# RWKV-7 recurrence with a SoLU block on one core: key scaling on VectorE, and a written order for the first half of the program

## The chip, the core and the metric

The kernel runs on one core of a Trainium2 chip. The core has five engines, each with its own in-order queue: TensorE (PE; its weight loads are shown as PEld), VectorE (DVE), ScalarE (ACT), GpSimd (POOL) and SyncE (SP), which here only issues DMA transfers. An instruction that waits for a semaphore holds everything behind it on its own engine and nothing on the others. The metric is the device time of one execution in microseconds, and its median over the runs shown.

## The reference

Two blocks follow each other. The first is a recurrence over 768 time steps for 4 batches and 8 heads with head size 40; the second is a feed-forward block with a SoLU activation, a layer norm and a second product, over the 3072 tokens that come out of the first.

```python
for t in range(S):                                   # S = 768, state is D x D, D = 40
    y[:, :, t] = einsum('bhd,bhde->bhe', rt, state)
    Sa = einsum('bhde,bhe->bhd', state, at)
    state_decay = state * wt[:, :, None, :] - einsum('bhd,bhe->bhde', Sa, bt)
    state = state_decay + einsum('bhd,bhe->bhde', vt, kt)
x = y.transpose(0, 2, 1, 3).reshape(B * S, H * D)    # (3072, 320)
h = x @ w_in                                         # (3072, 1024)
e = exp(h - max(h)); sm = e / (sum(e) + 1e-9)
solu = h * sm
ln = (solu - mean(solu)) / sqrt(var(solu) + 1e-6) * g_ln
out = ln @ w_out                                     # (3072, 320)
```

The weights `w_in`, `w_out` and `g_ln` come as 64-bit floats and the rest as 32-bit.

## The kernel before

**Chunks.** Time is cut into chunks of 64 steps. A work item i is one chunk of two batches, so that 128 partitions hold 2 x 64 steps; there are N = 24 items, and items i and i + 2 belong to the same two batches, whose state passes from one to the next. Inside an item the recurrence is a triangular system, solved by an explicit inverse of blocks of 32.

**What one item goes through**, with the line of the function in the code:

- its keys and values are loaded (`load_keys` L318 for w, b, a, k; `load_values` L328; `load_r` L335);
- the logarithm of the decays is summed along time on TensorE and exponentiated on ScalarE, once as `ei` and once inverted as `inv` (`logged` L349, `decay` L353);
- `scaled` (L386) multiplies the keys b and k by `inv` into the tile `kb`, with one GpSimd instruction for each of the two (L393);
- the a keys and the scaled b keys are transposed on TensorE (`front` L421, `front_b` L429), and `norm` (L465) multiplies them; its result `nt` is stored to DRAM;
- the results of two items together are read back as `blk` (`spread` L488) and inverted on VectorE (`invert` L495), in 30 steps that a schedule strews between other work. The first step is L502 to L508, and a late step is two products (L516) and two additions (L519). The inverse goes to DRAM (`uu_dram`, L525), and comes back for each item (`bring` L529) as `tu` and `uh`; `flip` (L542) transposes `tu` in 32 x 32 blocks on VectorE;
- `attend_kv`, `attend_r`, `scores`, `couple`, `close`, `carried`, `driven`, `solved`, `read` and `summed` (L574 to L711) make the item's output and its new state. `scores` has two maskings on VectorE (L444, `psi` and `lv`), `couple` multiplies by the flipped `tu`, `solved` has one masking (`lu`), `read` accumulates in two halves, `summed` and `leave` (L714) write the new state and store the output x through DRAM;
- `left` (L732) reads x back transposed, `hidden` (L740) multiplies it with `w_in` in five parts into the PSUM tile `h`, `highest` (L756) takes its maximum, `exped` (L763) the exponential on ScalarE, `weighed` (L771) the product with h on VectorE, `spreadof` (L780) the square on ScalarE and the power on GpSimd (L792), `folded` (L794) transposes the result on TensorE (`plnT`), and `output` (L845) multiplies it with `w2` (`po`) and stores it.

**The weights** are narrowed from 64 to 32 bits on the chip in 13 parts (5 of `w_in`, 8 of `w2`). A part is loaded by `land` (L161) and narrowed by `split` (L188) in three stages: the beginning on VectorE (L196, L197), the scaling on ScalarE (L199 to L206) and the end on VectorE (L208 to L210). When all are there, `centred` (L262) takes the mean out of `w2`.

**What sets the order.** The order of instructions on each engine is the order in which the Python code emits them. Four items are prepared first; then a loop runs over slots i = -1 to 26. In slot i the front of item i + 5 is made, item i + 1 is scored, item i is solved and read, and the feed-forward block works on item c = i - 2. From slot 5 on the slots have their steady form. The table `plans` (L896) says, slot by slot, where steps of inverses and stages of narrowing are strewn on VectorE; a number stands for so many steps, b, s and f for the three stages.

**Queues.** Most loads are issued from SyncE. GpSimd issues the loads of r, the stores of x and of most `nt`, the reads of most blocks, and a few of the early loads of b, a and k, all in one queue with its scalings. ScalarE issues the constants, the first b keys and the rows of g.

The scaling before is one line:

```python
for n in names:
    j = H * (n == "b")
    nc.gpsimd.tensor_tensor(out=kb[:, j:j + H, 0:D], in0=d["raw_" + n], in1=heads(d["inv"]), op=ALU.mult)
```

Of the kernel before, what the change touches and what calls it, by code (L numbers as in the profile page):

```python
# [17 lines left out]
P = 128  # L18
C = 64
# [9 lines left out]


# [23 lines left out]
def kernel(  # L54
# [93 lines left out]
    turn = dict(X="B", Y="C")  # L148

# [62 lines left out]
    begun, scaling, ended = [], [], []  # L212

    def begin_narrow():
        load, part = next(parts)
        assert load < len(lands) + 3 or len(ended) >= len(lands)
        begun.append((load, part, split(*part)))
        next(begun[-1][-1])

    def scale_narrow():  # L220
        scaling.append(begun.pop(0))
        next(scaling[-1][-1])

    def end_narrow():
        load, part, rest = scaling.pop(0)
        for _ in rest:
            pass
        ended.append(load)
        if part is landed[load][-1] and load in LANDS_NEXT:
            land(LANDS_NEXT[load], nc.gpsimd)  # L230

    def vector(plan):

        for word in plan.split():
            if word in "bsf":
                dict(b=begin_narrow, s=scale_narrow, f=end_narrow)[word]()
            else:
                some(int(word.strip("o")), (i + 2) // GRP if "o" in word else N)

    def turn_g(pg):  # L240
        nc.tensor.transpose(out=pg[:, 0:NF], in_=g_rows, identity=ident[0:NF, 0:NF])
        for x, y in zip(g_cols, (0, -20, -36)):
            nc.scalar.mul(out=x, in_=pg[:, 0:NF], mul=2.0 ** y)
# [7 lines left out]
    def mean_more(t, lo, hi, begun=None):  # L251
        if begun is not None:
            nc.tensor.matmul(t[:, 0:DM], lhsT=ident, rhs=begun, start=True, stop=False)
        mean_part(t, lo, hi, begun is None)
        return mean_kept(t)
# [85 lines left out]
    def by_value(i):  # L341
# [3 lines left out]
        for x, y in ((v_t[0][:, :, 0:D], d["lv"][:, :, C:]), (r_t[0][:, :, 0:D], d["raw_r"])):  # L345
# [7 lines left out]
    def decay(i, t=None):  # L353
# [3 lines left out]
        if "lw" not in d:  # L357
            logged(i)
# [3 lines left out]
        def evict():  # L362
            nc.scalar.activation(out=ei_t[0][:, :, 0:D], in_=heads(t), func=AF.Exp)
            inv = d["inv"] = two.tile([P, DM], FP32, tag="inv", name="inv", bufs=4)
            nc.scalar.activation(out=inv, in_=t, func=AF.Exp, scale=-1.0)
        return evict

    def decay_by_halves(i, t):
# [10 lines left out]
        def evict():  # L379
            nc.scalar.activation(out=ei_t[0].rearrange("p (x h) d -> p x h d", x=2)[:, :, :, 0:D],  # L380
                                 in_=t.rearrange("p x (h d) -> p x h d", d=D), func=AF.Exp)
            inv = d["inv"] = two.tile([P, DM], FP32, tag="inv", name="inv", bufs=4)
            nc.scalar.activation(out=inv.rearrange("p (x n) -> p x n", x=2), in_=t, func=AF.Exp, scale=-1.0)
        return evict

    def scaled(i, names="bk"):  # L386
# [4 lines left out]
        for n in names:  # L391
            j = H * (n == "b")
            nc.gpsimd.tensor_tensor(out=kb[:, j:j + H, 0:D], in0=d["raw_" + n], in1=heads(d["inv"]), op=ALU.mult)  # L393
# [65 lines left out]
    def shared_pair(i):  # L459

        if i not in shared:
            shared[i] = pair(turn["Y"], "py")
        return shared[i]

    def norm(i):  # L465
        if not ok(i):
            return
# [6 lines left out]
        nt = d["nt"] = tokens("nt", AHEAD)  # L474
        nc.scalar.mul(out=nt, in_=t[:, :, 4 * Q:4 * Q + 256].rearrange("p b (j c) -> p b j c", j=4), mul=-1.0)  # L475
        n, at = divmod(i, GRP)
        if at == 0:
            blocks[n] = dram.tile([2, 2 * GRP * H, Q, Q], FP32, tag="nt_dram", name="nt_dram")
        for x in range(2):
            for e in range(2):  # L480
                home = C * x + Q * e
                queue = nc.sync if 1 < i < 4 or i == 1 and x else nc.gpsimd
# [5 lines left out]
    def spread(n):  # L488
        nb = two.tile([P, Q, Q], FP32, tag="blk", name="blk")
# [3 lines left out]
        return nb  # L493

    def invert(n):  # L495
        u = two.tile([P, Q // 2, Q], FP32, tag="uu", name="uu")
        flat = u.rearrange("p c t -> p (c t)")
        nc.gpsimd.memset(u[C:P], 0.0)
        nc.gpsimd.memset(flat[C:P, 1::Q + 2], 1.0)
        nb = spread(n)  # L500
        yield
        nc.vector.tensor_tensor(out=u[0:C], in0=nb[0:C, 0::2], in1=above, op=ALU.mult)  # L502
        nc.vector.memset(flat[0:C, 0::Q + 2], 1.0)
        for j in range(1, Q - 1):
# [15 lines left out]
            if j < Q - 2:  # L520
                yield
        inverse[n] = dram.tile([Q, C, Q], FP32, tag="uu_dram", name="uu_dram")
        for y in range(2):
            queue = nc.sync
            queue.dma_start(out=inverse[n][y::2].rearrange("c b t -> b c t"), in_=u[C * y:C * y + C])  # L525
        yield


    def bring(i):  # L529
# [6 lines left out]
        for x in range(2):  # L536
            queue = nc.sync if i or not x else nc.gpsimd
            queue.dma_start(out=d["tu"][C * x:C * x + Q, :, Q:2 * Q], in_=src[0, at, :, x])
        for x in range(2):
# [21 lines left out]
    def close(i):  # L561
        if not ok(i):
            return
# [6 lines left out]
        nc.scalar.copy(out=d["tu"].rearrange("p (h j) c -> p h j c", h=2)[:, :, :, 2 * Q:],  # L570
# [3 lines left out]
    def attend_kv(i, t):  # L574
# [4 lines left out]
        for y, x in enumerate((d["kb"], v_t[0])):  # L579
            turned(t, y, x)  # L580
# [25 lines left out]
    def stated_r(i):  # L606

        if not ok(i) or not where_(i)[1]:
            return
# [6 lines left out]
        for x, part in enumerate((slice(0, HW), slice(HW, C))):  # L616
            nc.scalar.copy(out=state_of(i)[:, x, :, 0:part.stop - part.start].rearrange("p (x q) c -> p q x c", q=2),  # L617
                           in_=by_units(t[:, :, 0:256])[:, :, :, part])

    def scores(i):  # L620
# [3 lines left out]
        t = pair(turn["X"], "ps")  # L624
        for u in in_turn(lambda p, q, g, h: (h, p)):
            p, q, g, h = u
            j = 2 * q + g
            mm(t[half(p), h, j * C:j * C + C], keyed(d["kT"], u), keyed(d["aT"], u))
        for u in in_turn(lambda p, q, g, h: (q, p)):
# [3 lines left out]
        psi = d["psi"] = tokens("psi")  # L633
        masked(psi, by_units(t[:, :, 0:256]))
# [3 lines left out]
    def carried(i):  # L638
# [5 lines left out]
        d["px"] = pair(turn["X"], "px")  # L644
# [21 lines left out]
    def solved(i):  # L666

        if not ok(i):
            return lambda: None
        d = st[i]  # L670
        t = pair(turn["Y"] if i >= LAG else "h", "pu")
# [6 lines left out]
        copy = lambda: nc.scalar.copy(out=o[:, :, :, C:], in_=y[:, :, :, C:])  # L678
        if i < LAG:
            copy()  # L680
# [488 lines left out]
```

## Time and profile before

| | |
|---|---|
| runs, us | 538.32, 538.21, 536.38; median 538.21 |
| span of the profiled execution, us | 536.5 |
| TensorE busy | 480.7 us (90%) |
| VectorE busy | 430.6 us (80%), 1752 instructions |
| ScalarE busy | 314.1 us (59%) |
| GpSimd busy | 227.0 us (42%), 376 instructions |
| mean granted TensorE clock | 0.984 |
| DMA | 63.95 MB, mean 119 GB/s |

The page of a profile gives, for one execution, the busy time of each engine, the same in 40 slices of the span, the chain of work that ended last, followed back from the last instruction, and groups of equal instructions. A row of a group reads: line, engine, operation, output tile <- input tiles, output shape <- input shape and type, count | busy time, mean ns of one | idle time of the engine just before them, and what ended most of it. A row of the timeline reads: start, duration in us, engine, line, operation, tiles, shape, count, and in square brackets the idle time before it and who ended that. SPq and the like are the sequencers that issue DMAs. A duration can overlap the next one's start, so that the time from start to start is a little shorter. A row of the windows reads: stretch, length, and then for PE, PEld, DVE, ACT and POOL the busy time and the number of instructions, the granted clock, the share of the DMA engines, and GB/s. A row of the waits reads: who waited <- for whom: total us, times, longest.

The busy shares are averages over a beginning, in which items are prepared and weights narrowed, a steady part, and an end, so that stages are read apart in what follows.

### The profile page before, as it was taken

Reading aid. Unit: us, or ns where it says so; the run is one execution under the profiler, and the core shown is the slowest. Engines: PE = TensorE matmul, PEld = TensorE weight load, DVE = VectorE, ACT = ScalarE, POOL = GpSimd, SP = SyncE. Lnnn points to the kernel's source line nnn. Section 1 sums busy time; section 2 is a strip of 40 time slices with the busy share of each in tenths; the row PEclk is TensorE's granted clock in tenths of the full one; section 3 lists DMA queues with packets and bytes.
Section 4 is the critical chain, followed back from the end, with each engine's and each line's share of the span. In section 5 each row is a group of like instructions: output and inputs, shape, how many; then the busy total and the mean of one; then the engine's idle time right before and its main releaser. Section 6 shows DMA issues by size and latency. Waiting matters only on the chain.

```text
span 536.5 us, 28053 instructions
## 1 busy us (share of the span) xinstructions
PE 480.7 (90%) x12029; PEld 391.0 (73%) x12029; DVE 430.6 (80%) x1752; ACT 314.1 (59%) x627; POOL 227.0 (42%) x376
## 2 busy tenths in 40 slices
PE   4633775798989999999999999999999999999997
PEld 3522665665878878877887887788778877887766
DVE  4599987999997987997998979979989888544322
ACT  3633466488457566556666665666656555654433
POOL 4577538245253344545445263544445331210300
PEclk9999978799999999999999999999999999999999
DMA  8898889765465566674774776675554551421210
GB/s 149 153 157 160 177 142 206 165 134 124 90 131 120 102 125 138 123 151 96 147 156 104 132 150 121 118 155 109 114 118 102 108 111 43 106 65 29 61 53 24
DMA packets 194475, 63.95 MB, mean 119 GB/s; under 512 B 166840, under 2 KB 186528, under 8 KB 194352
## 3 DMA queue, kind: packets, MB, share of 16 engines
q1 hardware_dynamic: 181232, 41.60, 41.8%
q0 software_dynamic: 10768, 19.95, 15.2%
q8 instruction: 94, 1.54, 1.2%
q10 hardware_dynamic: 2352, 0.62, 0.7%
q14 instruction: 29, 0.24, 0.2%
HBM read 47.96 MB, written 14.16 MB: 116 GB/s over the span
## 4 chain that ended last, share of the span: by engine, by line
PE 73%; DVE 17%; DMA 5%; issue 2%; ACT 2%; SPq 0%; POOL 0%; ACTq 0%; POOLq 0%; DVEq 0%
PE po L285 20%; PE h L285 18%; PE px L285 6%; PE pyo L285 5%; PE py L285 5%; DVE prod L516 4%; PE ps L285 4%; DVE uu L519 3%; PE pu L285 3%; PE plnT L804 2%; PE pb L400 2%; PE pa L400 2%; PE psr L285 2%; PE pkv L400 2%; DMA uu_dram<-uu 1%
## 5 line engine op out<-in xcount | busy, mean ns | idle before, releaser
L285 PE MATMUL h<-w_in,xT 64*64 64x512 f32 (+1 forms) x1064 | 121.7, 551 | 0.7 <-issue 0.7
L285 PE MATMUL po<-w,lnT 128*128 128x160 f32 x768 | 115.2, 304 | 0.0
L516 DVE TENSOR_TENSOR prod<-blk,uu 128x48 f32<-128x48 f32 (+19 forms) x576 | 108.1, 227 | 1.3
L285 PEld LDWEIGHTS po<-w,lnT 128*128 128x128 f32 x768 | 105.5, 190 | 4.7 <-issue 0.8
L519 DVE TENSOR_TENSOR uu<-uu,prod 128x48 f32<-128x48 f32 (+19 forms) x576 | 103.8, 219 | 0.0
L483 POOL DMA_DIRECT2D nt_dram<-nt x86 | 50.8, 597 | 84.5 <-ACT nt L475 76.4
L792 POOL TENSOR_TENSOR rs<-var,mhalf 128x1 f32<-128x1 f32 x24 | 17.6, 734 | 138.2 <-ACT var L791 138.1
L761 DVE TENSOR_REDUCE nmax<-h 128x1 f32<-128x1024 f32 x24 | 29.3, 1219 | 32.9 <-PE h L285 32.9
L285 PEld LDWEIGHTS h<-w_in,xT 64*64 64x64 f32 x1064 | 36.7, 133 | 20.4 <-issue 16.7
L790 ACT ACTIVATE sq<-e,mu 128x1024 f32<-128x1024 f32 x24 | 26.9, 1119 | 24.4 <-DVE e L777 24.4
L444 DVE TENSOR_TENSOR lu<-pu,cst 128x512 f32<-128x512 f32 x24 | 16.5, 686 | 26.6 <-PE pu L285 24.8
L769 ACT ACTIVATE e<-h,nmax 128x1024 f32<-128x1024 f32 x24 | 26.7, 1111 | 17.7 <-DVE nmax L761 17.7
L558 ACT ACTIVATE wy<-py,cst 128x256 f32<-128x256 f32 x24 | 11.4, 474 | 39.2 <-PE py L285 37.1
L311 POOL DMA_DIRECT2D raw_r<-in_r_dram x48 | 33.3, 698 | 0.0
L777 DVE SCALAR_TENSOR_TENSOR e<-h,e 128x1024 f32<-128x1024 f32 x24 | 29.2, 1217 | 4.3 <-ACT e L769 4.1
L508 DVE SCALAR_TENSOR_TENSOR uu<-blk,uu 128x30 f32<-128x30 f32 (+3 forms) x144 | 30.2, 262 | 1.7 <-DMA blk<-nt_dram 0.8
L393 POOL TENSOR_TENSOR kb<-raw_b,inv 128x320 f32<-128x320 f32 x24 | 21.4, 894 | 21.1 <-DMA raw_b<-in_b_dram 13.7
L285 PE MATMUL pcum<-lw,cst 128*128 128x160 f32 x48 | 15.1, 461 | 16.7 <-ACT lw L351 16.7
L285 PEld LDWEIGHTS py<-tu,nt 64*64 64x64 f32 x768 | 17.3, 142 | 16.3 <-issue 10.7
L617 ACT COPY st<-psr 128x416 f32<-128x416 f32 (+1 forms) x44 | 14.2, 374 | 24.5 <-PE psr L285 24.4
L664 ACT ACTIVATE x<-px 128x832 f32<-128x832 f32 x24 | 20.7, 864 | 11.0 <-PE px L285 11.0
L710 DVE TENSOR_TENSOR tot<-pyo,st 104x416 f32<-104x416 f32 x44 | 23.8, 581 | 2.9 <-PE pyo L285 2.9
(154 smaller groups left out, 1095.3 us busy)
## 6 DMA issues: line engine op xcount, KB each, us to landing
xT<-x_dram SPq DMA_DIRECT2D x48, 160.0 KB, 4.2
blk<-nt_dram POOLq DMA_DIRECT2D x22, 256.0 KB, 4.7
raw_w<-in_w_dram SPq DMA_DIRECT2D x48, 80.0 KB, 3.3
raw_r<-in_r_dram POOLq DMA_DIRECT2D x48, 80.0 KB, 4.0
lv<-in_v_dram SPq DMA_DIRECT2D x48, 80.0 KB, 3.7
out_dram<-osb SPq DMA_DIRECT2D x46, 80.0 KB, 2.5
a<-in_a_dram SPq DMA_DIRECT2D x44, 80.0 KB, 4.0
raw_k<-in_k_dram SPq DMA_DIRECT2D x42, 80.0 KB, 3.8
```

The costliest lines, as they stand in the source:

```text
L285: nc.tensor.matmul(o, lhsT=lhsT, rhs=rhs, start=start, stop=stop, skip_group_check=True)
L311: queue.dma_start(out=x[half(p), :, 0:D], in_=ap[2 * bp + p, :, ci * C:(ci + 1) * C, :].rearrange("h t d -> t h d"))
L400: nc.tensor.transpose(out=t[0:W2, p, at + C * j:at + C * j + C], in_=x[half(p), 2 * j:2 * j + 2].rearrange("p a b -> p (a b)")[:, skip:ski ...
L483: queue.dma_start(out=blocks[n][e].rearrange("(a x h) s c -> a x s h c", a=GRP, x=2)[at, x], in_=nt[home:home + Q].rearrange("p h j c -> p ...
L508: nc.vector.scalar_tensor_tensor(out=u[:, c, j + 1:Q], in0=nb[:, j, j + 1:Q], scalar=u[:, c, j:j + 1], in1=u[:, c, j + 1:Q], op0=ALU.mult, ...
L516: nc.vector.tensor_tensor(out=ts[-1], in0=nb[:, j:j + 1, j + 1:Q].to_broadcast([P, hi - lo, m]), in1=u[:, lo:hi, j:j + 1].to_broadcast([P, ...
L519: nc.vector.tensor_tensor(out=u[:, lo:hi, j + 1:Q], in0=u[:, lo:hi, j + 1:Q], in1=x, op=ALU.add)
L710: nc.vector.tensor_tensor(out=by_b(tot)[:, :, :, part], in0=y[:, :, :, part], in1=by_b(state_of(i)[:, x])[:, :, :, 0:HW], op=ALU.add)
L761: nc.vector.tensor_reduce(out=nmax, in_=d["h"], axis=AX.X, op=ALU.max, negate=True)
L769: nc.scalar.activation(out=e, in_=d["h"], func=AF.Exp, bias=d["nmax"], accum_out=d["esum"])
L777: nc.vector.scalar_tensor_tensor(out=d["e"], in0=d["h"], scalar=1.0 / DFF, in1=d["e"], op0=ALU.mult, op1=ALU.mult, accum_out=d["mu"])
L790: nc.scalar.activation(out=pair("A" if i == N - 2 else "h", "sq").rearrange("p a b -> p (a b)"), in_=d["e"], func=AF.Square, scale=-float( ...
```

## The change

The change has two parts.

First, all 48 scalings of keys go from GpSimd to VectorE:

```diff
-            nc.gpsimd.tensor_tensor(out=kb[:, j:j + H, 0:D], in0=d["raw_" + n], in1=heads(d["inv"]), op=ALU.mult)
+            nc.vector.tensor_tensor(out=kb[:, j:j + H, 0:D], in0=d["raw_" + n], in1=heads(d["inv"]), op=ALU.mult)
```

Second, the code no longer emits instructions as it goes. It makes a list of 2,286 named pieces, in the old order, and then emits them sorted by their place in a written list, `ORDER`. Functions that did several things are cut for this: `summed` and `leave` into `summed`, `kept_state`, `answered` and `leave`; `scores` into one function for keys and one for values; every product on TensorE apart from its eviction, which is returned as a function.

```diff
+    def do(name, fn, *args):
+        seq.append((name, lambda: fn(*args)))
+
+    def do_pe(name, fn):
+        box = []
+        do(name, lambda: box.append(fn()))
+        return box
...
-        solved(i)()
-        vector(plan[1])
+        if ok(i):
+            box = do_pe(f"S{i}", lambda i=i: solved(i))
+            for x in (0, 1) if i < LAG else (1, 0):
+                evict(f"{'cm'[x]}lu{i}", box, x)
+        vector(plan[1], i)
...
-        scaled(j + 1, "b")
-        stated_r(i + 1)
+        scaled_(j + 1, "b")
+        if ok(i + 1) and where_(i + 1)[1]:
+            evict(f"Esr{i + 1}", do_pe(f"Sr{i + 1}", lambda i=i: stated_r(i + 1)))
...
+    place = {name: x for x, name in enumerate(ORDER.split())}
+    for name, piece in sorted(seq, key=lambda x: place.get(x[0], len(place))):
+        piece()
```

`ORDER` holds 1,107 names: the pieces from the first load to the end of slot 9, in which item 7 is in the feed-forward block. The pieces behind it keep their old order. Its beginning, and the stretch around the first hidden tiles:

```diff
+ORDER = """
+w0 b0 b1 w1 a0 lg0 Tc0 xi0 xe0 Tei0 sb0 Tb0 Ta0 L1 lg1 Tc1 Eei0 Ea0 v0 Eb0 xi1 xe1 N0 nt0 Tei1 Eei1 sb1 Tb1 a1 Ta1 Ea1
+L0 Eb1 N1 nt1 w2 lg2 a2 Tc2 nb0 k0 Z0 sn0 nb1 ns1 nf1 sn1q sk0 ns0 nf0 sn1 w3 xe2 b2 Z1 Ta2 xi2 B0 Tei2 Eei2 r0 Ea2
+lg3 Tc3 xi3 k1 sb2 i0.1 i0.2 i0.3 i0.4 i0.5 i0.6 Tb2 Eb2 i0.7 i0.8 xe3 Tei3 Eei3 i0.9 i0.10 i0.11 i0.12 w4 N2 nt2 a3
...
+nf4 nb6 Sk2 mk2 mv2 Ts2 sn5 S1 mlu1 nf5 nb7 Z2 lg7 Tc7 Es2 Sr2 ns6 Esr2 R0.1 K2 nf6 U1 xi7 sb6 clu1 nb8 R1.1 an1 sn4
+l0 H0.0 ks1 ns7 nf7 xe7 Tei7 ns8 nf8 b7 Tb6 Eb6 Eei7 Ta7 Ea7 r3 cr3 B2 i2.1 i2.2 i2.3 i2.4 H0.1 i2.5 i2.6 i2.7 i2.8 V2
+x0.2 H0.2 H0.3 i2.9 Tr3 Er3 uh2 N6 nt6 Ts3 Es3 Tmean0 Emean0 k4 Sr3 tu2 F2 C2 sk4 v3 cv3 w8 lg8 L11 L9 L10 H0.4 wy2
+Esr3 D2 tl2 Tk3 w9 Tv3 i2.10 i2.11 i2.12 lv1 i2.13 sb7 Ekv3 Tc8 xe8 xi8 i2.14 Sv3 nb9 m0 i2.15 tu3 Tei8 b8 ns9 nf9 Tb7
+Eei8 Sk3 mk3 mv3 Eb7 R0.2 S2 mlu2 e0 F3 K3 nb10 clu2 R1.2 i2.16 sb8 we0 ns10 nf10 a8 sn6 i2.17 t0.2 N7 i2.18 nt7 t1.2
...
+"""
```

The names: `w b a k v r` with a number are loads of that item's inputs, `L` a load of a part of the weights, `nb ns nf` the three stages of narrowing it; `lg Tc xi xe` the logarithm, the sums and the two exponentials of the decays; `sb sk` the scalings of b and k; `T..` transposes and `E..` their evictions (`Ea` and `Eb` of the a and b keys, `Eei` of the decays, `Ekv` and `Er` of keys, values and r); `N nt sn` the product of `norm`, its eviction and its store; `Z B` the clearing for an inverse and the read of its block; `i2.17` step 17 of inverse 2, `U` its store; `tu uh` what `bring` reads, `F` the flip; `C wy D tl` `couple` and `close`; `Sk mk Sv mv` the scores and their maskings; `S mlu clu` `solved`, its masking and its copy; `K V x0` `carried`, `driven` and the eviction; `R0 R1 t0 t1 ks an lv` the two halves of `read`, the sums, the new state, the output x and its store; `l H m e we sq rs` from `left` to the power of the feed-forward block; `Te Ee P Eo So` its transposes, output product and store.

More of the change, by code (lines that the diff above doesn't have):

```diff
@@ L488, in spread @@
     def spread(n):
-        nb = two.tile([P, Q, Q], FP32, tag="blk", name="blk")
+        nb = spreads[n] = two.tile([P, Q, Q], FP32, tag="blk", name="blk")
         for y in range(2):
@@ L868 @@
-    steps = []
-    def some(n, last=N):
-        while steps and steps[0][0] <= last and n:
-            if next(steps[0][1], steps) is steps:
-                steps.pop(0)
-            else:
-                n -= 1
-    parts = ((n, part) for n in range(len(lands) + NF) for part in landed[n])
-    def begin_inverse(n):
-        steps.append((n, invert(n)))
-        next(steps[-1][1])
-    for i in range(2):
-        load_keys(i, "w")
-        load_keys(i, "b", nc.scalar)
-        load_keys(i, "a")
@@ L1043 @@
+        if not steady and ok(i - 1):
+            do(f"l{i - 1}", left, i - 1)
         if i == EARLY - AHEAD:
-            load_keys(j + 3, "w")
+            keys(j + 3, "w")
         early = i < EARLY - AHEAD or i > N - 2
```

712 lines of the change are left out of this document (447 added, 265 removed).

## The prediction

> **What bounds the kernel now.** I read the windows by stage first, then the chain of waits, then the timeline of VectorE and TensorE before the steady part. In the windows the columns are the stretch, its length, and each engine's busy time with its instructions in brackets.
>
> ```profile
> 0.00:28.00 28.00, 15.10 (x192) 11.69 (x192) 14.38 (x40) 15.34 (x29) 12.81 (x43) 1.00 0.89 152
> 28.00:126.00 98.00, 62.94 (x1547) 51.07 (x1547) 92.19 (x413) 55.39 (x114) 53.58 (x81) 0.91 0.82 162
> 126.00:160.00 34.00, 32.72 (x897) 25.89 (x898) 32.86 (x131) 20.23 (x43) 15.99 (x25) 1.00 0.54 111
> 160.00:523.00 363.00, 360.32 (x9315) 293.31 (x9315) 288.12 (x1169) 218.35 (x432) 144.10 (x226) 1.00 0.53 109
> ...
> PE 73%; DVE 17%; DMA 5%; issue 2%; ACT 2%; SPq 0%; POOL 0%; ACTq 0%; POOLq 0%; DVEq 0%
> ```
>
> From 160 to 523 us TensorE is busy 360.3 of 363 us: that part is TensorE's own work, and nothing on another engine shortens it. Before 126 us TensorE is busy only 78.0 of 126 us (15.10 + 62.94). From 28 us on it is VectorE that has no room: 92.2 of 98 us. So the kernel is a full TensorE program that begins too late, and VectorE's order of work up to about 130 us decides how late. The 17% of VectorE in the chain lies there. The question is how much earlier TensorE's unbroken stretch can begin.
>
> Where it begins, and what held it:
>
> ```profile
> 25.80 0.68 DVE L502 TENSOR_TENSOR uu<-blk,above 64x512 f32<-64x512 f32 x1 [0.71 <-DMA blk<-nt_dram]
> 27.41 2.83 DVE L508 SCALAR_TENSOR_TENSOR uu<-blk,uu 128x30 f32<-128x30 f32 x12 [0.78 <-DMA blk<-nt_dram]
> ...
> 119.97 1.22 DVE L761 TENSOR_REDUCE nmax<-h 128x1 f32<-128x1024 f32 x1
> ...
> 123.60 1.21 DVE L777 SCALAR_TENSOR_TENSOR e<-h,e 128x1024 f32<-128x1024 f32 x1
> ...
> 126.16 0.71 PE L804 MATMUL plnT<-cst,e 64*128 64x64 f32 x16 [1.67 <-ACT sq L790]
> ...
> 132.64 0.43 DVE L546 STREAM_TRANSPOSE tu<-tu 128x256 f32<-128x256 f32 x1
> ...
> 137.98 0.62 PE L285 MATMUL py<-tu,nt 64*64 64x32 f32 x32
> ```
>
> VectorE weighs the first hidden tile (L777) at 123.6 us. The transposes of it (L804) wait for that and for the square on ScalarE until 126.16. VectorE's flip of chunk 4 (L546) is done at 133.07, but TensorE, held at 126.16, comes to the product that reads it only at 137.98, 4.9 us later. From then on it does not stop. After the flip of chunk 4, then, 4.9 us could be won without VectorE doing anything sooner, and more if the flip itself came sooner.
>
> **The change, part by part.** Called with its pieces in their old order, the new program issues the old sequence on TensorE, ScalarE and SyncE, and on VectorE and GpSimd the old one but for the 48 key scalings. So there are two parts: the scalings change engine, and the order of pieces up to the end of slot 9 is new.
>
> *The order at the first weighing.* In the new order, ahead of L777 of chunk 0 on VectorE, these no longer stand: steps 17 to 30 of inverse 2, two beginnings and one end of a narrowed part, and the two sums of chunk 2. A late step takes two pairs of instructions:
>
> ```profile
> 37.69 0.34 DVE L516 TENSOR_TENSOR prod<-blk,uu 128x60 f32<-128x60 f32 x2
> 37.95 0.34 DVE L519 TENSOR_TENSOR uu<-uu,prod 128x60 f32<-128x60 f32 x2
> 38.22 0.34 DVE L516 TENSOR_TENSOR prod<-blk,uu 128x56 f32<-128x56 f32 x2
> ...
> 121.11 0.32 DVE L196 TENSOR_SCALAR scale<-bits 128x320 int32<-128x320 int32 x1
> 121.34 0.32 DVE L197 TENSOR_SCALAR w<-bits 128x320 int32<-128x320 int32 x1
> ...
> 122.60 1.08 DVE L710 TENSOR_TENSOR tot<-pyo,st 104x416 f32<-104x416 f32 x2
> ```
>
> That is 37.69 to 38.22, 0.53 us a step: 14 x 0.53 = 7.4, plus 2 x 0.47 for the beginnings, about 1.4 for the end (three instructions of the length of L196 to L710's halves, an estimate) and 1.0 for the sums: 10.7 us of VectorE moved behind the weighing. TensorE is no longer held there. The next thing that can hold it is the flip of chunk 4. Ahead of that flip the two orders have nearly the same VectorE work: one step of inverse 3 has gone behind it, one maximum (1.22 us, L761) has come before it, less than 1 us together. So of the 10.7 us only the 4.9 between flip and product are won: **-4.9**. Unless the flip itself comes sooner, the rest is lost in waiting for it.
>
> *The scalings.* What one costs on GpSimd, and what it does to VectorE:
>
> ```profile
> L393 POOL TENSOR_TENSOR kb<-raw_b,inv 128x320 f32<-128x320 f32 x24 | 21.4, 894 | 21.1 <-DMA raw_b<-in_b_dram 13.7 <-DMA g_rows<-in_moe_g_ln_dram 4.0 <-ACT inv L365 3.0
> ...
> 43.22 0.97 DVE L519 TENSOR_TENSOR uu<-uu,prod 128x30 f32<-128x30 f32 x2
> 43.28 0.85 POOL L393 TENSOR_TENSOR kb<-raw_b,inv 128x320 f32<-128x320 f32 x1
> 44.10 1.69 POOL L393 TENSOR_TENSOR kb<-raw_k,inv 128x320 f32<-128x320 f32 x2
> 44.22 1.62 DVE L516 TENSOR_TENSOR prod<-blk,uu 128x28 f32<-128x28 f32 x2
> ...
> 45.98 0.30 DVE L516 TENSOR_TENSOR prod<-blk,uu 128x21 f32<-128x21 f32 x2
> ```
>
> Pairs that take 0.30 us alone took 0.97 and 1.62 while GpSimd scaled three times: 0.67 + 1.32 = 2.0 us, 0.66 a scaling. VectorE stands still while GpSimd scales. The Trainium skill, page "SBUF — State Buffer", section "SBUF: two separate sides", has the rule: a VectorE instruction with two inputs in SBUF and a GpSimd one that reads SBUF exclude each other for a whole instruction. The trace agrees, with 0.66 of the 0.89 us; by the rule's full length the sum below would be 14 x 0.23 = 3 us better.
>
> From 28 to 126 us there are 14 scalings on GpSimd:
>
> ```profile
> 28.00:120.00 92.00, 13.39 (x14) 0.91 0.83 164
> ...
> L210 DVE TENSOR_TENSOR w<-w,bits 128x320 f32<-128x320 f32 x8 | 3.9, 494 | 0.3
> ...
> L444 DVE TENSOR_TENSOR psi<-ps,cst 128x512 f32<-128x512 f32 x24 | 16.4, 684 | 1.6 <-PE ps L285 1.3
> ```
>
> They take away up to 14 x 0.66 = 9.2 us of VectorE, and nothing if none of them meets a two-input instruction; VectorE is busy 94% of that stretch, mostly with such instructions, so I take 9.2. The price on VectorE is not in the trace; the same shape (L210) takes 0.49 us, of which some 0.05 overlaps the next, so 0.45. From above L444 bounds it, 0.68; from below the start-to-start time of L196, 0.23. In the new order 16 scalings stand ahead of flip 4, of which four stand ahead of inverse 0, where VectorE idles (28 - 14.38 = 13.6 us): 12 x 0.45 = 5.4, bounds 2.8 to 8.2. Net **-3.8**, bounds -6.4 to +8.2. In the steady part the rest costs nothing: 48 - 14 = 34 scalings at most, 34 x 0.45 = 15 us, lie in VectorE's 363 - 288.1 = 74.9 us of idle time, and stalls go there too. Without that cover it would be 15 us.
>
> *Waits at flips.*
>
> ```profile
> 81.27 1.58 SPq L525 DMA_DIRECT2D uu_dram<-uu  x2
> ...
> 94.06 0.45 DVE L546 STREAM_TRANSPOSE tu<-tu 128x256 f32<-128x256 f32 x1 [2.69 <-DMA tu<-uu_dram]
> ...
>   DMA tu<-uu_dram: 3.5, 4
> ```
>
> From the unloading of an inverse to the flip of its first chunk took 12.8 us here, and VectorE, which works in order, stood 2.69 us. In the new order some 17 us of VectorE work (the ends of five narrowed parts, nine steps of inverse 2, aT, masks and products between) stand between inverse 1 and flip 2: **-2.7**, lower bound 0. Between inverse 2 and flip 4, though, there are only some 9 us (two answers, two states, two beginnings, two ends, three masks, one scaling, one maximum). A new wait of 0 to 12.8 - 9 = 3.8 us; I take **+1.5**: all 24 flips together waited 3.5 us for their transfers, flip 2 alone 2.69 of it, and the others had about 10 us of work between.
>
> *Queues at the start.* Each SyncE load issues in 0.65 us. The b keys of chunk 2 move from 12.23 us to behind the store of block 1 and a w load, and the block's read behind them; the last column of the page's row on raw_k is the median time to landing:
>
> ```profile
> 12.23 1.30 SPq L311 DMA_DIRECT2D raw_b<-in_b_dram  x2
> ...
> 18.00 1.18 SPq L483 DMA_DIRECT2D nt_dram<-nt  x2
> 19.22 1.28 SPq L311 DMA_DIRECT2D raw_w<-in_w_dram  x2
> ...
> raw_k<-in_k_dram SPq DMA_DIRECT2D x42, 80.0 KB, 3.8
> ```
>
> So the b load issues from 19.22 + 1.28 = 20.5 to 21.8 and lands near 25.6, and its scaling stands ahead of inverse 0 on VectorE, which began at 25.80: **+0.8**, bounds 0 to 3, since the a keys of chunk 1 too now stand behind a w_in part and the values of chunk 0, four more issues of 0.65. Behind that scaling stands all of inverse 0, for which everything waits. GpSimd, in turn, issues its own loads without scalings between them, which only helps.
>
> Sum: -4.9 - 3.8 - 2.7 + 1.5 + 0.8 = -9.1 us. The profiled span is 536.5 us; the three runs are 536.38, 538.21 and 538.32, so the span lies 1.7 below their median. I take the difference from the median: 538.2 - 9.1 = **529.1 us**, own range 525 to 533.5.
>
> **The rivals.**
>
> B, *the flips hold it*. If the 12.8 us round trip holds at flips 4, 6 and 8, where I count 9, 8 and 9 us of VectorE work between, VectorE stands 3.8 + 4.8 + 3.8 = 12.4 us instead of 1.5, of which some 3 are covered where TensorE still has work (an estimate): 529.1 + 8 = 537. For it: flip 2 waited. Against: the other 23 flips waited 3.5 - 2.69 = 0.8 us in all.
>
> C, *slower: loads stop VectorE*. GpSimd waited for keys, and nobody minded:
>
> ```profile
> POOL kb L393 <- DMA raw_b<-in_b_dram: 13.7, 2, 7.7
> ...
> POOL kb L393 <- DMA raw_k<-in_k_dram: 4.7, 2, 3.7
> ```
>
> Now such a wait stops inverses, masks and flips behind it. If these 18.4 us come back on VectorE ahead of flip 4 the time is 529.1 + 18.4 = 547.5; it is slower than before from 9.1 us on, so 539 to 547, middle 543. Against: the new order issues the loads of k0, b3 and the later keys well ahead of their scalings, and GpSimd's queue is shorter.
>
> D, *faster still: TensorE quick from the start*.
>
> ```profile
> 62.20 1.65 PE L285 MATMUL px<-lv,psi 64*64 64x104 f32 x32
> ...
> 119.00 0.94 PE L285 MATMUL px<-lv,psi 64*64 64x104 f32 x32
> ```
>
> The same 32 matmuls took 1.65 us after a pause and 0.94 in a dense stretch. If a denser start makes them quick, VectorE's other 3.1 us of waiting (98 - 92.19 - 2.69) go too, and with them the 1.5: 529.1 - 4.6 = 524.5. The Trainium skill, page "TensorE: Matmul & The Clock Gate", section "What's actually happening", says that TensorE runs at half clock after about 3.4 us of idling. By that rule D follows from any order that leaves no such gap. The durations agree; the granted clock, 0.91 over the stretch, shows less than half of it.
>
> E, *the stall is not the scaling's*. One also stands under GpSimd's issue of a DMA:
>
> ```profile
> 47.15 0.69 POOL L311 DMA_DIRECT2D a<-in_a_dram  x1
> 47.24 1.37 DVE L502 TENSOR_TENSOR uu<-blk,above 64x512 f32<-64x512 f32 x1
> ```
>
> L502 took 0.68 at 25.80 and 1.37 here, with no scaling near. If all stalls are of that kind they stay, the change does not free VectorE, and the -9.2 is gone: 538.3.
>
> **How the numbers follow.** Forecast 0.56, B 0.13, C 0.16, D 0.10, E 0.05. A measurement of this kernel can tell about 0.5% (2.7 us) from no change. Faster by more: the forecast, D, and 0.06 of B: 0.72. Within: 0.07 of B and E: 0.12. Slower: C, 0.16. The range goes from below D, 523.5, to past E, 538.5, and leaves out C and little of D. It holds the bounds of the price of a scaling (12 x 0.23 more is +2.8) and of the new wait.
>
> **What would show it.** Right: VectorE's group L516 mean falls from 227 ns; a scaling on VectorE takes 0.42 to 0.52 us; the weighing of chunk 0 comes near 105 us and flip 4 near 128, with couple(4) on TensorE straight behind it; TensorE idles less before 126 us and no more after 160. Wrong: VectorE waits for raw_b, raw_k or tu in the tens of us (C, B); stalls of 0.66 us that stay (E); flip 4 early but its product late, which would mean that TensorE or ScalarE holds the start and not VectorE; or new idle time of TensorE behind slot 9.

## The result, and the profile after

The changed kernel takes 532.86 us (median of four runs, 532.62 to 535.16), the kernel before 538.27 in the same session. The ratio is 0.9908, with a 95% interval of 0.9878 to 0.9937, so 5.0 us are won (3.4 to 6.6). The forecast was 529.1. Timed again beside other kernels, the change gave 0.9902 (0.9868 to 0.9937). The profiled execution is the slowest of the four: 535.16 us, span 533.3.

The windows of the changed kernel, with the columns as before, and the line of its chain of waits:

```profile
0.00:28.00 28.00, 12.92 (x150) 10.09 (x151) 14.62 (x39) 13.16 (x25) 12.11 (x45) 1.00 0.96 163
28.00:126.00 98.00, 75.62 (x1852) 58.96 (x1848) 91.74 (x436) 63.33 (x130) 41.24 (x67) 0.97 0.78 153
126.00:160.00 34.00, 33.05 (x787) 27.75 (x789) 31.72 (x141) 20.68 (x44) 11.14 (x20) 0.95 0.67 133
160.00:523.00 363.00, 359.66 (x9198) 292.13 (x9195) 280.90 (x1185) 212.57 (x422) 115.19 (x197) 1.00 0.53 109
...
PE 77%; DMA 8%; DVE 7%; ACT 3%; SPq 3%; issue 2%; DVEq 0%; ACTq 0%
```

TensorE does 88.5 us of work before 126 us (12.92 + 75.62) where it did 78.0, and VectorE's share of the chain falls from 17% to 7%. That is the shape which the prediction wanted. VectorE is as full as before from 28 to 126 us (91.7 us for 92.2): what it gained it filled with other work.

The timeline of the changed kernel at the start, at the first weighing and at the flip of chunk 4 (VectorE's row of the flip ahead of TensorE's rows):

```profile
27.11 0.49 DVE L428 TENSOR_TENSOR kb<-raw_b,inv 128x320 f32<-128x320 f32 x1 [2.18 <-DMA raw_b<-in_b_dram]
28.59 0.68 DVE L546 TENSOR_TENSOR uu<-blk,above 64x512 f32<-64x512 f32 x1 [0.99 <-DMA blk<-nt_dram]
...
108.62 1.22 DVE L850 SCALAR_TENSOR_TENSOR e<-h,e 128x1024 f32<-128x1024 f32 x1
...
111.67 0.71 PE L883 MATMUL plnT<-cst,e 64*128 64x64 f32 x16
...
128.28 0.43 DVE L590 STREAM_TRANSPOSE tu<-tu 128x256 f32<-128x256 f32 x1
...
127.64 1.43 PE L286 MATMUL pmean<-mean,cst 128*128 128x320 f32 x2
128.87 2.31 PE L282 MATMUL pmean<-w,cst 128*128 128x320 f32 x4
131.11 0.67 PE L318 MATMUL py<-tu,nt 64*64 64x32 f32 x32
```

The weighing of chunk 0 comes 15.0 us earlier (123.60 to 108.62), the flip of chunk 4 4.4 us earlier (132.64 to 128.28), the product that reads it 6.9 us earlier (137.98 to 131.11). TensorE no longer waits at `plnT`: its row has no bracket.

What the scalings cost on VectorE, and what became of VectorE's stalls, in the groups of the changed kernel:

```profile
L428 DVE TENSOR_TENSOR kb<-raw_b,inv 128x320 f32<-128x320 f32 x24 | 11.4, 474 | 4.7 <-ACT inv L398 2.5 <-DMA raw_b<-in_b_dram 2.2
L428 DVE TENSOR_TENSOR kb<-raw_k,inv 128x320 f32<-128x320 f32 x24 | 11.4, 482 | 0.0
L563 DVE TENSOR_TENSOR uu<-uu,prod 128x48 f32<-128x48 f32 (+19 forms) x576 | 94.2, 204 | 0.0
L560 DVE TENSOR_TENSOR prod<-blk,uu 128x48 f32<-128x48 f32 (+19 forms) x576 | 93.9, 204 | 1.2
```

The two groups of the inverses had means of 227 (`prod`) and 219 ns (`uu`) before; 576 x (23 + 15) = 21.9 us are gone from them. The engine of the scalings decides this and not the order: with the scalings alone on VectorE the means are 202 and 203 ns, with the order alone 212 and 220.

The lead does not last. The table gives the start of the output product (`po`) of five chunks in us, from timelines of TensorE (two of the rows, of the change, stand under the experiments). The last column is the lead in a second profile of the change, taken later.

| chunk | before | change | lead | lead, second profile |
|---|---|---|---|---|
| 0 | 142.23 | 135.11 | 7.1 | 4.1 |
| 2 | 181.83 | 172.75 | 9.1 | 5.4 |
| 3 | 200.53 | 193.54 | 7.0 | 4.9 |
| 5 | 238.59 | 234.33 | 4.3 | 1.8 |
| 9 | 312.63 | 308.99 | 3.6 | 1.2 |

The leads differ from one execution to the next, but both go the same way: behind chunk 2 some 4 to 5 us are lost (9.1 to 3.6, 5.4 to 1.2), nearly all of it ahead of chunk 6, in slots that the new order still arranges.

### The profile page after: what moved, and what is told of

Read it like the earlier page. It is cut to its first block, busy times and chain, and to the rows that moved or that the text cites. A ratio compares the mean times of both kernels' runs of the same rounds, so it can differ in the third digit from the quotient of the medians.

```text
span 533.3 us, 28056 instructions
## 1 busy us (share of the span) xinstructions
PE 487.6 (91%) x12029; PEld 394.7 (74%) x12029; DVE 420.0 (79%) x1800; ACT 313.1 (59%) x627; POOL 180.2 (34%) x328
## 4 chain that ended last, share of the span: by engine, by line
PE 77%; DMA 8%; DVE 7%; ACT 3%; SPq 3%; issue 2%; DVEq 0%; ACTq 0%
PE po L318 19%; PE h L318 18%; PE py L318 6%; PE pyo L318 6%; PE px L318 6%; PE ps L318 4%; PE pu L318 3%; DMA a<-in_a_dram 3%; PE plnT L883 2%; PE pkv L435 2%; PE psr L318 2%; PE pb L435 2%; PE pa L435 2%; SPq L344 2%; DVE prod L560 1%
## 5 line engine op out<-in xcount | busy, mean ns | idle before, releaser
L560 DVE TENSOR_TENSOR prod<-blk,uu 128x48 f32<-128x48 f32 (+19 forms) x576 | 93.9, 204 | 1.2
L563 DVE TENSOR_TENSOR uu<-uu,prod 128x48 f32<-128x48 f32 (+19 forms) x576 | 94.2, 204 | 0.0
L318 PEld LDWEIGHTS h<-w_in,xT 64*64 64x64 f32 x1064 | 38.9, 133 | 24.9 <-issue 20.6
L871 POOL TENSOR_TENSOR rs<-var,mhalf 128x1 f32<-128x1 f32 x24 | 13.7, 571 | 119.4 <-ACT var L863 119.1
L802 POOL DMA_DIRECT2D x_dram<-x x24 | 18.0, 750 | 37.9 <-DVE x L793 37.7
L552 DVE SCALAR_TENSOR_TENSOR uu<-blk,uu 128x30 f32<-128x30 f32 (+3 forms) x144 | 26.9, 242 | 2.5 <-DMA blk<-nt_dram 1.9
L629 ACT COPY kvT<-pkv 104x1024 f32<-104x1024 f32 x24 | 24.2, 1010 | 6.7 <-PE pkv L435 6.4
L318 PE MATMUL pu<-x,tu 64*64 64x104 f32 x768 | 25.9, 265 | 0.7 <-ACT bT L445 0.5
L318 PE MATMUL px<-lv,psi 64*64 64x104 f32 x768 | 24.2, 264 | 2.2 <-DVE lv L479 2.2
```

Source lines behind the costliest of these rows:

```text
L318: nc.tensor.matmul(o, lhsT=lhsT, rhs=rhs, start=start, stop=stop, skip_group_check=True)
L552: nc.vector.scalar_tensor_tensor(out=u[:, c, j + 1:Q], in0=nb[:, j, j + 1:Q], scalar=u[:, c, j:j + 1], in1=u[:, c, j + 1:Q], op0=ALU.mult, ...
L560: nc.vector.tensor_tensor(out=ts[-1], in0=nb[:, j:j + 1, j + 1:Q].to_broadcast([P, hi - lo, m]), in1=u[:, lo:hi, j:j + 1].to_broadcast([P, ...
L563: nc.vector.tensor_tensor(out=u[:, lo:hi, j + 1:Q], in0=u[:, lo:hi, j + 1:Q], in1=x, op=ALU.add)
L629: return lambda: nc.scalar.copy(out=o[0:W2].rearrange("p b j t -> p b (j t)"), in_=t[0:W2])
```

## Experiments

In each, a ratio is to the kernel before, run beside it, with its 95% interval. Times of the kernel before were 536.4 to 538.4 us in these sessions.

**Each half alone.** The first keeps the scalings on VectorE and empties the list, the second keeps the list and puts the scalings back.

```diff
 # the scalings alone
-ORDER = """
-...
-"""
+ORDER = """"""
 # the order alone
-            nc.vector.tensor_tensor(out=kb[:, j:j + H, 0:D], in0=d["raw_" + n], in1=heads(d["inv"]), op=ALU.mult)
+            nc.gpsimd.tensor_tensor(out=kb[:, j:j + H, 0:D], in0=d["raw_" + n], in1=heads(d["inv"]), op=ALU.mult)
```

> The scalings on VectorE, every piece in the order of the kernel before. Theory 1 (both halves pay, as the sum said: order -4.9, scaling -3.8): 533.5 to 535.5 us, about 4 below before; the stalls of 0.66 us gone, the weighing of chunk 0 still holding TensorE (product of chunk 0 near 139 us, between 142.2 of before and 135.1 of the change). Theory 2 (the scaling alone carries the gain, the order adds nothing): 532.5 to 533.5, the same as the change. Theory 3 (VectorE is not the bound before 126 us, the order carries everything): 537.5 to 539.

> The new order, the scalings back on GpSimd with their stalls. Theory 1: the order's 4.9 less what the slots behind the fifth give back (some 5 us as the change's trace reads), so 536 to 540 us. Theory 2: no better than before, 537 to 540, with the product of chunk 0 no earlier than 140 us. Theory 3 (the order carries everything): 532.5 to 534.5.

Measured: the scalings alone 537.41 us, 1.0008 (0.9991 to 1.0026); the order alone 542.88 us, 1.0101 (1.0068 to 1.0134). Neither half pays, and the order by itself makes the kernel slower. So all three theories fall: the first, since the halves do not add; the second and third, since each named a half that carries the gain. The order alone came out slower than any of the three had it.

The windows and VectorE's two longest waits from 28 to 126 us, of the run with the scalings alone:

```profile
28.00:126.00 98.00, 65.02 (x1547) 53.63 (x1547) 86.27 (x423) 54.16 (x111) 37.79 (x64) 0.79 0.78 159
```

```profile
DVE kb L385 <- DMA raw_k<-in_k_dram: 5.2, 2, 3.6
DVE tu L547 <- DMA tu<-uu_dram: 3.2, 1, 3.2
```

VectorE has 5.9 us less to do there than before (86.27 for 92.19), and TensorE is no further: 65.02 us busy for 62.94, at a lower granted clock (0.79 for 0.91), with the same 1547 instructions. VectorE stood 5.2 us for loads of k; before, such waits were GpSimd's. Whether they are what holds this run, the next one asks.

**The loads' waits in the old order.** The scalings of k for chunks 5 and 6 were put behind `x0.0` and `x0.1`, in the old order with the scalings on VectorE. The list of this run names the whole old order; it differs from it in these places:

```diff
-F0 sb5 N4 nt4 sn4 sk5 cv1
+F0 sb5 N4 nt4 sn4 cv1
...
-V0 x0.0 Tc6
+V0 x0.0 sk5 Tc6
...
-Z2 B2 sk6 cv2
+Z2 B2 cv2
...
-V1 x0.1 R1.0
+V1 x0.1 sk6 R1.0
```

> The order of before, the scalings on VectorE, and only the two scalings of k for chunks 5 and 6 moved back, each behind the state rows of chunk 0 and 1, since VectorE waited 3.6 and 1.6 us for their loads with the scalings alone moved. Theory 1 (those waits at the head of VectorE's queue ate what the stalls had cost): 533 to 535 us, flip of chunk 1 near 66 to 68 us against 70.7. Theory 2 (VectorE does not set the end in the old order, TensorE's hold and half clock do): 536 to 538, the flips earlier and the product of chunk 0 still near 143 to 145 us.

Measured: 536.66 us, 0.9981 (0.9962 to 1.0001). VectorE no longer waits for k from 28 to 126 us. The flip of chunk 1 came at 70.2 us, the product of chunk 0 at 140.8. That is 1.4 us better than the scalings alone by the two ratios, and the two intervals overlap: theory 2 has the time, though it put that product near 143 to 145 us. So the waits for k are at most a part of what ate VectorE's freed time in the old order. What the rest is stays open.

**Where the new order gives its lead back.** In four kernels the list was cut: only the pieces that had come first in the old order keep their place in it, and all others follow in the old order. The list itself was written out shorter in these runs; this is what it amounts to, with the count for the cut in slot 5:

```diff
+    first = {name for name, _ in seq[:853]}
-    place = {name: x for x, name in enumerate(ORDER.split())}
+    place = {name: x for x, name in enumerate(n for n in ORDER.split() if n in first)}
```

The counts were 571 (to `Tc10`, the sums of the decays of chunk 10), 787 (to `Tc13`), 853 (to `P3`, the output product of chunk 3) and 1032 (to `P5`). What the expectations call the load of chunk 10 or 13 is this `Tc`.

> The change with its order kept only for the pieces that stood ahead of the load of chunk 10 in the kernel before (before the products of chunk 0). Theory A: the weighing of chunk 0 still comes near 109 us and the product of chunk 0 near 136 us, 528 to 531 us. Theory B: 532 to 534. Theory C: over 534, the wait at flip 4 back.

> The change with its order kept for the pieces that stood ahead of the load of chunk 13 in the kernel before (to the products of chunk 2), and the order of before from there. Theory A (the 5 us that TensorE loses from 182 to 250 us are the new order's in those slots): 527 to 529.5 us, product of chunk 6 near 248 to 250 us against 253.2. Theory B (the lead is given back at any place where the new order ends and the old one goes on, since pieces brought forward are only owed): 532 to 534, the product of chunk 6 near 253. Theory C (the slots are needed in that order, and are worse without): over 534.

> The change itself, timed beside the three kernels that follow. All theories: 531 to 534 us, ratio to before near 0.991.

> The new order ended at the load of chunk 13, beside the change on one chip. Theory A (slots 5 to 9 of the new order give back 4 to 5 us): 3 to 5 us under the change, ratio to before 0.983 to 0.988, on every pair of runs. Theory B (its 526.97 us was one lucky start, 3 us early by the product of chunk 0): median within 1.5 us of the change.

> The new order kept one slot longer, to the pieces ahead of the products of chunk 3 in the kernel before. Theory A, with the loss spread over slots 5 to 9: 527.5 to 531.5 us, between the cut at chunk 13 and the change. Rival, that the loss is at the flip of chunk 8 alone (the chain runs there from VectorE through the inverse's last flip and its two DMAs to TensorE): as the change, 531 to 534, if the pieces of that flip are inside, or as the cut at chunk 13 if not.

> The order kept to the products of chunk 3, scalings on VectorE, beside the two kernels that follow. 526 to 530 us, ratio to before 0.976 to 0.984; product of chunk 3 to product of chunk 5 in 37 to 38 us.

> The order kept to the pieces ahead of the products of chunk 5, scalings on VectorE. Theory A (the loss lies between the products of chunk 3 and 5, which took 40.8 and 41.2 us in the change, 38.1 before and 37.7 with the order ended at chunk 3): 531.5 to 534, as the change, and that stretch near 41 us. Rival (the loss is a little in each slot, or behind the product of chunk 5): 528 to 530.5, the stretch near 38.

| list kept to | median, us | ratio | product 3 to product 5, us |
|---|---|---|---|
| `Tc10` | 533.73 | 0.9943 (0.9922 to 0.9963) | 36.9 |
| `Tc13` | 530.05 | 0.9870 (0.9836 to 0.9903) | 37.3 |
| `Tc13`, again | 530.27 | 0.9852 (0.9818 to 0.9886) | 37.1 |
| `P3` | 528.11 | 0.9797 (0.9756 to 0.9838) | 37.7 |
| `P3`, again | 528.21 | 0.9824 (0.9788 to 0.9861) | 37.2 |
| `P5` | 530.13 | 0.9876 (0.9838 to 0.9914) | 39.8 |
| slot 9 (the change, again) | 533.1 | 0.9902 (0.9868 to 0.9937) | 41.2 |
| nothing (before) | | 1 | 38.1 |

The last column is the difference of two rows such as these, of the change and then of the list kept to `P3`:

```profile
193.54 1.62 PE L318 MATMUL po<-w,lnT 128*128 128x160 f32 x10
...
234.33 1.90 PE L318 MATMUL po<-w,lnT 128*128 128x160 f32 x12
```

```profile
192.76 1.49 PE L307 MATMUL po<-w,lnT 128*128 128x160 f32 x9
...
230.50 1.76 PE L307 MATMUL po<-w,lnT 128*128 128x160 f32 x11
```

The kernel with the shorter list is 0.8 us ahead at the first and 3.8 us ahead two chunks later. With the list ended at `P3`, 528.1 and 528.2 us, the kernel beats both the change (533.1 in the same session, intervals apart) and the kernel before, by 1.8 to 2.0%. It is the best version found, 5 us under the change. The list kept to `Tc10` loses its lead where it is cut: the products of chunks 0 and 1 stand 29.0 us apart there, 20.2 in the change. So theory B holds for a cut at the wrong place. The later cuts are nearer to theory A, whose ranges both runs of `Tc13` missed by less than 1 us (530.05 us for at most 529.5, and 2.8 us under the change for at least 3). With the list kept to `P5` the time, 530.13 us, lies in the rival's range, and the stretch, 39.8 us, between the two: a part of the loss comes with the pieces up to `P5`, and a part with those behind them. That the flip of chunk 8 alone makes the loss, the rival of the run with `P3`, is not excluded by that run, whose interval overlaps that of `Tc13`; but the list kept to `P5` has that flip and by its median loses only part.

**The fourth corner.** With the list ended at `P3`, the scalings went back to GpSimd, by the same edit as in the order alone.

> The same order with the scalings back on GpSimd: with before, the scalings alone and the run beside this it makes the four corners. Theory 1 (the order's saving at the first weighing, 4.9 us, stands by itself once slots 6 to 9 are left as they were): 531.5 to 534.5 us, 4 to 6 below before. Theory 2 (the new order lives on VectorE's freed time, as the new order alone, 1% slower, suggests): 536 to 541, no better than before, the product of chunk 0 near 138 us but those behind it later.

Measured: 541.58 us, 1.0071 (1.0041 to 1.0102), a little beyond what theory 2 said, and far from theory 1. The scalings' engine is worth nothing in the old order (1.0008), and in this one 2.5% (1.0071 to 0.9824), some 13 us. Up to the product of chunk 0 the run with the scalings on GpSimd is not behind: 136.70 us, against 134.97 and 138.06 in the two profiles with them on VectorE. It falls back between the products of chunks 0 and 5, which stand 103.7 us apart in it and 95.5 and 94.6 in the others. In that stretch there are 12 scalings. With 0.66 us each they could stall VectorE for 7.9 us, and VectorE is idle 15 of the 86 us from 136 to 222, so that stalls are unlikely to be all of the loss. The waits of GpSimd from 60 to 250 us show something else, in the kernel before, then in this order with the scalings on GpSimd, then with them on VectorE:

```profile
POOL kb L393 <- DMA raw_k<-in_k_dram: 3.7, 1, 3.7
```

```profile
POOL kb L417 <- DMA raw_k<-in_k_dram: 33.7, 6, 12.1
POOL nt_dram L514 <- ACT nt L502: 17.8, 4, 5.0
```

```profile
POOL nt_dram L514 <- ACT nt L502: 45.7, 8, 9.6
POOL x_dram L791 <- DVE x L782: 23.7, 3, 17.6
```

Before, GpSimd waited 3.7 us for k in this stretch. In the new order it waits 33.7 us (40.0 with the whole list), and behind these waits stand its stores of x and of `nt`. The chain of waits of the run with the scalings on GpSimd shows one such case, with start, duration and what:

```profile
142.08 4.99 DMA raw_k<-in_k_dram
...
147.21 0.92 POOL kb L417
148.13 0.69 POOL x_dram L791
148.82 0.58 POOL x_dram L792
149.40 3.44 DMA x_dram<-x
...
154.26 0.62 SPq L333
154.88 0.04 issue
154.93 3.71 DMA a<-in_a_dram
158.64 0.04 issue
158.68 0.65 PE pa L424 x15
```

A load of k lands late, GpSimd scales it, only then issues the store of x, SyncE reads x back and only then issues a load of a, and TensorE starts on that a at 158.68. TensorE's time in the windows from 136 to 200 us, on GpSimd and on VectorE:

```profile
136.00:200.00 64.00, 59.05 (x1540) 49.71 (x1532) 56.44 (x266) 37.20 (x78) 28.73 (x46) 0.99 0.67 124
```

```profile
136.00:200.00 64.00, 63.27 (x1623) 54.19 (x1616) 59.51 (x280) 40.37 (x82) 23.53 (x40) 0.99 0.66 132
```

TensorE idles 4.9 us in the first and 0.7 in the second.

**The wait without the work.** To the kernel with the list ended at `P3` and the scalings on VectorE, a small instruction was added on GpSimd at each scaling, whose result nothing reads:

```diff
             nc.vector.tensor_tensor(out=kb[:, j:j + H, 0:D], in0=d["raw_" + n], in1=heads(d["inv"]), op=ALU.mult)
+            nc.gpsimd.tensor_tensor(out=probe, in0=d["raw_" + n][:, 0, 0:1], in1=d["inv"][:, 0:1], op=ALU.mult)
```

> The order kept to the products of chunk 3 with the scalings on VectorE, and at each scaling's place one small multiplication on GpSimd of one column of the same two operands into a scrap tile: GpSimd waits again for every load of k and b, and works on it for a fraction of the 0.9 us that a scaling took there. Theory Q (what the scalings cost in the new order is their wait for k at the head of GpSimd's queue, ahead of the stores of x and of nt, 33.7 us of it from 60 to 250 us with the scalings on GpSimd): most of the loss comes back, 534 to 541 us, ratio to before 0.995 to 1.007, GpSimd waiting 25 to 40 us for raw_k before that multiplication. Theory S (it is the time of the scalings on GpSimd and the stalls that they put on VectorE): 527 to 530 us, ratio 0.978 to 0.986, as without it.

The row on the tile of that instruction (shortest, median and longest in ns, first and last start in us), and GpSimd's waits from 60 to 250 us:

```profile
L420 POOL TENSOR_TENSOR probe<-raw_k,inv x24: 181/204/597, 20.4 to 399.2; 128x1 f32<-128x1 f32 x24
```

```profile
POOL probe L420 <- DMA raw_k<-in_k_dram: 35.1, 6, 9.6
POOL nt_dram L517 <- ACT nt L505: 21.5, 6, 5.6
```

Measured: 533.98 us, 0.9921 (0.9887 to 0.9954). The wait for k is back (35.1 us for 33.7), the work is not (0.20 us at the median for 0.9). The trace shows what one such wait holds up:

```profile
135.49 0.75 DVE L785 TENSOR_TENSOR x<-tot,ex 104x256 f32<-104x256 f32 x2
143.66 0.19 POOL L420 TENSOR_TENSOR probe<-raw_k,inv 128x1 f32<-128x1 f32 x1 [5.66 <-DMA raw_k<-in_k_dram]
144.25 0.72 POOL L794 DMA_DIRECT2D x_dram<-x  x1 [0.40 <-DVE uu L555]
150.36 1.30 SPq L333 DMA_DIRECT2D a<-in_a_dram  x2
155.56 0.86 PE L427 MATMUL pa<-cst,a 64*104 64x64 f32 x8 [3.20 <-DMA a<-in_a_dram]
```

VectorE is done with x at 136.24 us, its store is issued 8 us later, behind the small multiplication, and at the end TensorE stands 3.20 us for a. Without that instruction, in the second run of the list ended at `P3`, x is done at 141.31 and its store is issued at 141.60.

The time lies at the lower bound of theory Q; the ratio lies between the ranges of the two. From 0.981 (the middle of the two runs without it, in other sessions) to 0.992 is 1.1%, of the 2.6% to 1.0071: the waits at the head of GpSimd's queue are some four tenths of what the scalings cost there, 6 us (three tenths to more than half by the interval of this run). These are all of GpSimd's waits at those places, for `inv` (10.5 us from 60 to 250 us) and b as well as for k. The other six tenths come with the work itself, GpSimd's time and VectorE's stalls, which were not told apart.

## Why the prediction was right, and where it was not

**Right: where the gain is.** TensorE's full stretch does begin earlier, and VectorE's order no longer holds it at the first weighing. The weighing was expected near 105 us and came at 108.62, flip 4 near 128 and came at 128.28. The wait at flip 2 is gone, as priced (-2.7), and the new one at flip 4 (+1.5) did not come: VectorE waited for `tu` once in the whole run, 1.0 us. At the product behind flip 4, where the sum ends, the work came 6.9 us earlier in this profile and 8.3 in the second, for the 9.1 of the sum. That the lead is 9.1 us at the product of chunk 2 is luck: in the second profile it is 5.4.

**Right: the price of a scaling.** 0.42 to 0.52 us on VectorE were expected, 0.474 and 0.482 measured. The stalls went with the scalings: 204 ns for both groups of the inverses. The rule of the Trainium skill, page "SBUF — State Buffer", section "SBUF: two separate sides", that was weighed there, agrees with these means. The count of 14 scalings was read from a row that ends at 120 us; to 126 us there are 15, which would make the 9.2 us 9.9.

**Off: the product behind flip 4.** It was to follow straight behind the flip, which was done at 128.71, and came at 131.11, 2.4 us later. The six matmuls of `pmean` ahead of it took 1.43 and 2.31 us, while the change's second profile shows them in 0.81 and 1.24 at a granted clock of 1.00: that is 1.7 us of the 2.4. The windows of the first profile around them show the clock:

```profile
124.00:126.00 2.00, 1.39 (x78) 1.11 (x69) 2.00 (x5) 1.88 (x5) 1.86 (x4) 1.00 0.48 89
126.00:127.60 1.60, 0.96 (x35) 0.87 (x35) 1.57 (x4) 0.59 (x1) 1.04 (x2) 1.00 0.67 136
127.60:131.10 3.50, 3.50 (x13) 1.85 (x6) 1.98 (x5) 0.00 (x1) 0.00 (x0) 0.51 0.79 147
```

The granted clock was 0.51 there, though TensorE had been busy 2.35 of the 3.6 us ahead of it, with a longest pause of 1.06 us. The Trainium skill, page "TensorE: Matmul & The Clock Gate", section "What's actually happening", gives half clock after about 3.4 us of idling; here it came behind a stretch that was one third idle. Rival D was tied to long gaps by that rule; in this place shorter ones stood ahead of the half clock.

**Off: the start.** Inverse 0 began 2.8 us later (25.80 to 28.59), not 0.8, within the bounds of 0 to 3, for the reason given: a wait for raw_b (2.18) and one for the block. Whether it is a part of the 3.6 us by which the weighing came later than expected is not shown; in the second profile the inverse began at 26.97 and the weighing came at 109.46.

**The step that failed first: the sum.** It added -4.9 for the order and -3.8 for the scalings as if each stood alone. Alone the scalings change the time by 0.0008 of it, within the noise, and the order costs 1.0% (5.4 us). Together they win 0.9%. So the time fell into the stated range by a sum of which neither term holds alone, and that is luck in part. In their profiles the order alone did bring the product of chunk 0 forward by 4.0 us (142.23 to 138.26), near its term, and had lost that by chunk 4 (218.99 to 220.87); the scalings alone did not bring it forward at all (144.55). The term for the scalings was worked out on VectorE alone, by the stalls that they remove and the instructions that they add, and of GpSimd's queue the text said that it now "issues its own loads without scalings between them, which only helps", and priced that at nothing. In the new order the scalings' engine is worth about 2% (1.0101 to 0.9905, the middle of the change's two ratios), against 0.7% for the 3.8 us. GpSimd's queue has a part in that: the new order waits for k on GpSimd ahead of the stores of x and `nt`, and with the scalings on VectorE it does not. With the shorter list those waits were some 6 us of 13; how the rest divides between GpSimd's time and VectorE's stalls is open.

**The second: "From then on it does not stop".** The sum ended at the product behind flip 4 and was carried from there to the end as it stood. But the list arranges the slots up to slot 9, and from chunk 2's product on it gives back 5.4 of 9.1 us in one profile and 4.2 of 5.4 in the other. With the list ended at `P3` the kernel keeps its lead and takes 528.1 and 528.2 us, 1 us under the forecast: the total of the sum is what that kernel does, though its terms were not what made it, so that this too is luck. What in those slots of the list costs the time is open: from 200 to 240 us TensorE was busy 38.9 us with 984 matmuls in the change, 40.0 us with 1137 where the list ends at `P3` (38.5 with 979 and 40.0 with 1068 in the second profiles), and no single wait was found that carries the loss.

**The rivals.** B, the flips: VectorE's only wait for `tu` in the changed kernel is 1.0 us long. C, loads stopping VectorE: 2.2 us for raw_b in all, none for raw_k. The mechanism of C exists all the same, in the other corners: on VectorE in the old order (5.2 us), on GpSimd in the new. E, stalls that are not the scaling's: refuted by the 204 ns, against 212 and 220 with the order alone. D, TensorE quicker: the granted clock from 28 to 126 us rose from 0.91 to 0.97, but the time stayed above the forecast.

## What to carry over

When an instruction changes engine, price both queues: the waits that it made at the head of the queue that it leaves, with the stores and loads behind them, have a price of their own. Here they cost some 6 us, about as much as the whole change won. Two edits that were worked out together need four corners, not a sum; here the corners are 1, 1.0008, 1.0101 and 0.9905. And follow a lead to the end of what the change arranges: a table of one milestone per chunk showed within one trace where it was lost, and cutting the change there won 5 us more.

## What was not expected of the hardware

Some of the stalls in the kernel before stood under GpSimd's DMA issues with no scaling near, such as L502 at 47.24 us, 1.37 us long. They went too, though GpSimd still issues: in the changed kernel the same instruction took 0.68 us under two such issues.

```profile
52.26 0.59 POOL L582 DMA_DIRECT2D tu<-uu_dram  x1 [3.60 <-DMA uu_dram<-uu]
52.55 0.68 DVE L546 TENSOR_TENSOR uu<-blk,above 64x512 f32<-64x512 f32 x1
52.84 2.71 POOL L344 DMA_DIRECT2D raw_k<-in_k_dram  x4
```

Even the 48 small multiplications on GpSimd brought none back. The group of the products in that run:

```profile
L552 DVE TENSOR_TENSOR prod<-blk,uu 128x48 f32<-128x48 f32 (+19 forms) x576 | 93.4, 202 | 1.2
```

Why a stall could show beside an issue alone was not settled; the spans on GpSimd are rough.

Kernels with the same beginning also differ from one execution to the next: in seven profiles with this list, scalings on VectorE and a cut no earlier than `Tc13`, the product of chunk 0 began between 129.5 and 138.2 us. One place where they part is in the products of `close` for chunk 4, here in the change's second profile:

```profile
131.07 0.49 PE L318 MATMUL py<-uh,wy 64*64 64x32 f32 x21
134.27 0.53 PE L318 MATMUL py<-uh,wy 64*64 64x32 f32 x10 [2.71 <-issue]
```

TensorE stops in the middle of 32 equal matmuls for 2.71 us, and the profile shows nothing that it waits for. Two others of the seven have this stop, with 2.13 and 1.89 us. Its cause is open.
